# Routed attention and a SoLU layer on one core: the first pair's values loaded later, eight score tiles kept in a weight's place, and another order of the first 50 microseconds

## The chip, the core and the metric

The kernel runs on one core of a Trainium2 chip. A core has a matrix engine (TensorE, called PE), a vector engine (VectorE, DVE), an engine for activation functions (ScalarE, ACT), a general engine (GpSimd, POOL) and an engine that here only starts DMAs (SyncE, SP). Each takes its instructions in the order in which they were issued to it; between engines they wait on semaphores. Data lies in SBUF (128 partitions) and, for the results of PE, in PSUM (banks of 512 f32 for each partition). The metric is the device time of one execution, in microseconds (us); smaller is better.

## The reference

Four batches, eight heads, 768 tokens, head dimension 64. Each query and each key is assigned to the nearest of 16 centroids of its head; a query attends only to keys of its own cluster. The result goes through a layer with a softmax-weighted activation and a layer norm.

```python
q_assign = argmax(einsum('bhsd,hcd->bhsc', q_n, c_n))     # k_assign likewise; c_n: centroids at unit length
mask = q_assign[:, :, :, None] == k_assign[:, :, None, :]
attn = softmax(where(mask, q @ k.T / sqrt(64), -1e9))
x = (attn @ v)                                            # as 3072 tokens x 512
h = x @ w_in                                              # 512 x 1024
solu = h * softmax(h)
out = ((solu - mean) / sqrt(var + 1e-6) * g_ln) @ w_out   # 1024 x 512
```

## The kernel before

The kernel works on pairs of heads, `b.p` (batch, pair): 0.0 is the first pair. All its work is cut into small named pieces, and the class `Weave` holds, for each engine, a hand-written queue of the kinds of pieces (`ORDER`). A piece of a kind is taken in the order in which it was added. `AWAY` moves single pieces from their default engine to another. So the order of every engine's instructions is fixed text; the costs given to `add` only serve to merge the queues into one program.

The pieces of batch 0, in the order of one pair's life, with their lines:

- `ld`, `lv` (SP): the DMAs of queries and keys (`load_tokens` L367 for pair 0.0, `load_apart` L373 for the other three) and of values (`load_v` L526). `lo`, `li`, `lg` (SP) load w_out, w_in and g_ln. In the kernel before, the DMA of the first pair's values stands fixed in the code at L811, behind the loads of pair 0.0.
- `tp` (PE, L383): three f32 transposes of a half of q or k into one of the three banks of the PSUM region `hreg`, which the pieces use in turn. `xa` (DVE or ACT, L390) copies that bank out to `xt`; the third `tp` behind waits for it. `tp0.1.1.0` is pair 0.1, side 1 (keys; 0 is queries), half 0.
- `ca` (POOL, ACT or DVE, L424): casts `xt` to bf16 in `qk`.
- `cl` (PE, L439), `tb`, `mx`, `oh`, `ot` (all DVE, L457 to L495): scores against the centroids, transposed back, maximum, one-hot, transposed. Pair 0.0 has these twice, one for each half of its tokens. `pl` (POOL or DVE, L499) places the one-hot rows below the cast rows of `qk`; `bl` (L522) blanks 16 rows. `cp`, `cb`, `cq`, `cf` make two forms of the centroids; `zo` clears a tile once.
- `S` (PE, L595): one bank of scores, 128 keys x 384 queries (pair 0.0) or 512 columns (the others), into one of three PSUM banks; it needs the `E` three banks before. `S4.0` is bank 0 of unit 4. Banks 0 to 23 are pair 0.0 (units 0 to 3), S4.0 is bank 24.
- `E` (ACT, L604): the exponential of that bank into a bf16 tile `e`. There are 9 such tiles, so the tenth `E` waits for the `V` that read the first.
- `V` (PE, L616): six matmuls of one 128-query block with the values in `v1`, which `cv` (POOL or DVE, L532) cast and `z` (POOL) completed. `N` (DVE, L629) divides by the sum; the next group's `V` waits for it, since there is one PSUM tile `ops`.
- `su`, `me` (PE), `sk`, `ce` (DVE): sums and centring of w_out. `wi` (POOL, L552): casts one 128-row slice of w_in, 128x1024, to `w_in_sb`. `h`, `y` (PE, L709, L763) are the two matmuls of the second layer, `hm`, `u`, `bn` (DVE) and `ex` (ACT) its activation. `fl` and `wm` (PE, L818) are matmuls on zeros that nobody reads.

From about 46 us on, scores, values and the second layer are interleaved up to the end.

Of the kernel before, what the change touches and what calls it, by code (L numbers as in the profile page):

```python
# [22 lines left out]
class Weave:  # L23
# [6 lines left out]
        ld4 lv si ld4 lv lg ld4 lv2 ld4 lo2 ld4 lo ld3 lo ld3 li4 tx ld3 lv3 tx ld4 tu ld9 lv ld tu  # L30
        tx ld3 tu ld3 ou ld2 ou ld tu ld12 tu ld4 lv ld2 ou tx ld3 tu ou ld2 tx lv ld tu ld4 tx ld
        tu ou2 ld lv ld4 tu ld4 tu ld ou ld7 pl ou ld lv2 ld3 tu lv tx ou tu lv pl ld4 ou2 tx lv tu
        tx ou tu pl2 tu2 tx tu tx ou2 tx ou tu tx2 ou tu2 ou2 tu2 ou6
    """
    ORDER["POOL"] = """
        po z ca2 pl2 cv z bl pl2 ca z ca pl2 ca z2 ca3 cv ca cv ca pl3 sg ca cv2 pl3 ca2 gs pl ca cv
        ca wi ca pl2 wi3 bl ca pl2 cv at cv pl ca pl al bl at cv ca pl ca pl cv ca3 al at ca al ca
        at ca pl2 bl cv pl2 ca4 at ca2 al ca pl2 bl pl2 cv2 ca3 al at pl2 bl pl2 ca pl al ca3 at cv
        at pl ca pl2 ca2 pl al cv2 bl cv2 pl2 ca pl al pl at al at pl2 ca3 at al bl cv pl2 bl cv2
# [130 lines left out]
def kernel(  # L170
# [15 lines left out]
    P = 128  # L186
# [1074 lines left out]
```

## Time and profile before

| | |
|---|---|
| median of three runs | 225.12 us (225.0 to 227.68) |
| the profiled execution | 225.3 us |
| its span, first to last instruction | 223.3 us (2.0 us lie around it) |
| PE, DVE, ACT, POOL busy | 216.1, 196.8, 192.0, 127.7 us |
| granted PE clock | 0.999 |

How to read it: the times are of one execution. A row gives the start, the time, the engine, the line of the code, the operation, the tile written and the tiles read, the number of instructions, and in brackets how long the engine had been idle before and what ended that. Neighbours with the same form are merged into one row. A busy PE is not PE at its peak: a matmul's row holds the way through the array too, so a single matmul of 384 columns shows 0.33 us where a chain of them advances by 0.16 to 0.17 us.

### The profile page before, as it was taken

How to read it: one execution, taken by the hardware profiler on the slowest of the kernel's cores; microseconds unless marked ns; L12 is line 12 of the kernel's file. 1: busy time of each engine (PE TensorE's matmuls, PEld its weight loads, DVE VectorE, ACT ScalarE, POOL GpSimd, SP SyncE). 2: the span in 40 equal slices, each digit the busy share in tenths (PEclk: the TensorE clock that was granted, in tenths of full speed). 3: DMA queues.
4: the chain of work that ended last, by engine and by line, in shares of the span. 5: the costliest groups of instructions: out<-in, count | busy, mean ns of one | idle time of the engine just before them, and what ended most of it. 6: DMA issues, size and time to landing. Idle time of an engine off the chain costs nothing.

```text
span 223.3 us, 6607 instructions
## 1 busy us (share of the span) xinstructions
PE 216.1 (97%) x2420; PEld 147.7 (66%) x2420; DVE 196.8 (88%) x359; ACT 192.0 (86%) x372; POOL 127.7 (57%) x247
## 2 busy tenths in 40 slices
PE   6899999999999999999999999999999999999994
PEld 2576656677667678776577667777677777755452
DVE  3899898899999989999998999887999889888982
ACT  3689999999998999998889899999999998983362
POOL 3489843864794999547678534943895403022331
PEclk9999999999999999999999999999999999999999
DMA  7997999999897989898999999299930534486723
GB/s 152 330 310 156 259 186 270 274 265 192 143 214 137 220 142 162 170 191 182 188 243 150 152 187 216 72 219 191 235 63 15 92 61 129 93 145 159 181 85 120
DMA packets 125679, 38.80 MB, mean 174 GB/s; under 512 B 115016, under 2 KB 121168, under 8 KB 125648
## 3 DMA queue, kind: packets, MB, share of 16 engines
q1 hardware_dynamic: 123904, 37.87, 79.6%
q10 hardware_dynamic: 1744, 0.52, 1.0%
q8 instruction: 19, 0.31, 0.6%
q14 instruction: 12, 0.10, 0.1%
HBM read 23.11 MB, written 6.29 MB: 132 GB/s over the span
## 4 chain that ended last, share of the span: by engine, by line
PE 88%; ACT 5%; issue 2%; DMA 2%; DVE 1%; SPq 1%; POOL 0%; ACTq 0%; DVEq 0%; POOLq 0%
PE sps L602 28%; PE hreg L711 19%; PE yps L775 17%; PE ops L625 15%; PE csc L451 4%; ACT e L608 4%; DMA raw<-in_q_dram 2%; PE hreg L387 1%; PE hreg L575 1%; PE hreg L775 1%; PE csc L446 1%; SPq L370 0%; ACT xt L394 0%; PE hreg L585 0%; PE utp L699 0%
## 5 line engine op out<-in xcount | busy, mean ns | idle before, releaser
L608 ACT ACTIVATE e<-sps 128x512 bf16<-128x512 f32 (+1 forms) x294 | 151.0, 598 | 12.1 <-PE sps L602 10.2
L602 PE MATMUL sps<-qk 80*128 80x256 bf16 (+5 forms) x636 | 93.8, 264 | 1.7 <-POOL qk L515 0.7
L602 PEld LDWEIGHTS <-qk 80*128 80x128 bf16 (+1 forms) x636 | 60.2, 121 | 27.9 <-issue 9.0
L625 PEld LDWEIGHTS <-e 128*128 128x128 bf16 x1152 | 50.4, 97 | 12.3 <-issue 1.9
L625 PE MATMUL ops<-v,e 128*128 128x65 bf16 x1152 | 55.0, 193 | 0.0
L711 PE MATMUL hreg<-w_in_sb,xT 128*128 128x512 bf16 x192 | 52.9, 379 | 0.0
L775 PE MATMUL yps<-w_out_c,uT 128*128 128x512 bf16 x184 | 48.5, 379 | 0.0
L730 DVE TENSOR_TENSOR u<-e_sb,hreg 128x1024 bf16<-128x1024 bf16 (+1 forms) x25 | 29.1, 1168 | 5.2 <-ACT e_sb L723 5.1
L515 POOL COPY qk<-oht 32x384 f32<-32x384 f32 (+1 forms) x50 | 24.9, 498 | 15.3 <-DVE oht L495 13.0
L741 DVE BATCH_NORM_STATS2 bs<-u 128x6 f32<-128x512 bf16 x48 | 31.5, 677 | 0.1
L717 DVE TENSOR_REDUCE nmax<-hreg 128x1 f32<-128x1024 f32 x24 | 29.0, 1210 | 2.6 <-PE hreg L711 2.2
L723 ACT ACTIVATE e_sb<-hreg,nmax 128x1024 bf16<-128x1024 f32 x24 | 26.9, 1120 | 4.5 <-DVE nmax L717 4.4
L434 POOL CAST qk<-xt 64x768 bf16<-64x768 f32 (+1 forms) x31 | 25.9, 837 | 5.1 <-DVE xt L394 3.6
L775 PEld LDWEIGHTS <-uT 128*128 128x128 bf16 x200 | 18.3, 97 | 11.8 <-issue 0.3
L757 POOL TENSOR_SCALAR esq<-es,mv 128x1 f32<-128x1 f32 x24 | 8.6, 358 | 29.2 <-DVE mv L745 21.0
L436 POOL TENSOR_SCALAR qk<-xt 64x768 bf16<-64x768 f32 (+1 forms) x28 | 23.0, 822 | 1.7
L711 PEld LDWEIGHTS <-xT 128*128 128x128 bf16 x192 | 16.7, 97 | 9.4 <-issue 0.6
L408 DVE STREAM_TRANSPOSE xt<-raw 128x768 f32<-128x768 f32 x24 | 22.6, 953 | 0.3 <-DMA w_g<-in_moe_w_out_dram 0.2
L751 POOL TENSOR_SCALAR es<-esum 128x1 f32<-128x1 f32 x24 | 5.3, 223 | 25.9 <-ACT e_sb L723 25.4
L650 DVE TENSOR_TENSOR x<-ops,den 128x256 bf16<-128x256 f32 (+1 forms) x39 | 18.9, 486 | 1.3
L533 POOL CAST v<-vf 128x384 bf16<-128x384 f32 x27 | 13.6, 518 | 2.2 <-DMA vf<-in_v_dram 1.5
L760 POOL TENSOR_TENSOR alpha<-esq,halves 128x1 f32<-128x1 f32 x24 | 13.5, 563 | 2.0
(80 smaller groups left out, 164.5 us busy)
## 6 DMA issues: line engine op xcount, KB each, us to landing
vf<-in_v_dram SPq DMA_DIRECT2D x16, 384.0 KB, 4.9
out_dram<-y SPq DMA_DIRECT2D x23, 256.0 KB, 2.6
raw<-in_q_dram SPq DMA_DIRECT2D x50, 96.0 KB, 3.6
raw<-in_k_dram SPq DMA_DIRECT2D x50, 96.0 KB, 3.1
w_g<-in_moe_w_out_dram SPq DMA_DIRECT2D x4, 512.0 KB, 5.2
w_st<-in_moe_w_in_dram SPq DMA_DIRECT2D x4, 512.0 KB, 6.1
raw<-in_q_dram SPq DMA_DIRECT2D x3, 384.0 KB, 6.2
raw<-in_k_dram SPq DMA_DIRECT2D x3, 384.0 KB, 6.9
```

Of the source, the lines that this page charges most:

```text
L434: VEC[e].tensor_copy(dst, src)
L436: VEC[e].tensor_scalar(dst, src, scalar1=inv_C, scalar2=1.0, op0=Alu.mult, op1=Alu.mult)
L515: ins = VEC[e].tensor_copy(dst.bitcast(F32), src.bitcast(F32).unsqueeze(1) .to_broadcast([NB, 2, n // 2]))
L602: nc.tensor.matmul(sps_[n, k][:, c0:c0 + w], side(b, h // 2, 1, h % 2, keys)[r], side(b, h // 2, 0, h % 2, slice(s0 * P, s0 * P + w))[r])
L608: nc.scalar.activation(es[n, k][:, :w], sps_[n, k][:, :w], Act.Exp, scale=exp_scale, bias=-exp_scale)
L625: nc.tensor.matmul(opss[g][:, s, :VW], es[n, k][:, c0:c0 + P], v1[slot(b, h // 2)][:, h % 2, kt, :VW], start=(kt == 0), stop=(kt == n_t - 1))
L711: uses(nc.tensor.matmul(hreg[:, at(f, f2)[1], :], xTs[f][:, dc, :], w_in_sb[:, dc, f2 * FF2:(f2 + 1) * FF2], start=(dc == 0), stop=(dc == ...
L717: uses(nc.vector.tensor_reduce(ff[f, "nmax"][:], pair_of(f), axis=AXY, op=Alu.max, negate=True), *both(f))
L723: uses(nc.scalar.activation(ff[f, "e"][:], pair_of(f), Act.Exp, bias=ff[f, "nmax"][:], accum_out=ff[f, "esum"][:]), *both(f))
L730: uses(nc.vector.tensor_tensor(ff[f, "u"][:, at_], ff[f, "e"][:, at_], pair_of(f)[:, at_], op=Alu.mult), *banks)
L741: nc.vector.bn_stats(ff[f, "bs"][:, f2, :], ff[f, "u"][:, f2, :])
L775: ins = nc.tensor.matmul(dst, ff[f, "uT"][:, at(f, f2)[0] * (n_fc // 2) + c, :], w_out_c[:, fc, cols], start=(fc == chunks[0]), stop=(fc = ...
```

## The change

1. The DMA of the first pair's values is no longer fixed behind the loads of pair 0.0; it is a piece of SP's queue (`lv0.0`), and stands behind the loads of pairs 0.1 and 0.2.
2. The exponentials of banks 0 to 7 no longer go to the 9 tiles `e`, but to the eight 128x512 halves of `w_in_sb`, which stands empty until `wi` fills it. So the first `E` that waits for a `V` is the eighteenth. Each `wi` now waits for the `V` of the units whose banks lie there.
3. The queues of all five engines have another order up to about S19.0, and some pieces another engine. Behind that point all queues are what they were.

What the queues hold up to bank 24, spelled out (PE from the first scores, DVE from the first token copies, ACT from its first copies, POOL):

```
PE before   ... cl0.0.1 fl x4 S0.0 S0.1 S0.2 tp0.1.0.0 tp0.1.0.1 S1.0 S1.1 tp0.1.1.0 S1.2 cq S0.3 tp0.1.1.1 S0.4 S0.5
            tp0.2.0.0 tp0.2.0.1 S1.3 S1.4 V0.0-2 S1.5 cl0.1 S2.0 tp0.2.1.0 tp0.2.1.1 V1.0-2 S2.1 gt S2.2 tp0.3.0.0 S2.3
            tp0.3.0.1 S2.4 S2.5 cl0.2 S3.0 S3.1 V2.0 V2.1 S3.2 V2.2 S3.3 S3.4 tp0.3.1.0 S3.5 S4.0 tp0.3.1.1 S4.1
PE after    ... cl0.0.1 fl x3 tp0.1.0.0 tp0.1.0.1 S0.0 S0.1 S0.2 cq tp0.1.1.0 tp0.1.1.1 S1.0 S1.1 S1.2 tp0.2.0.0
            tp0.2.0.1 S0.3 S0.4 cl0.1 S0.5 S1.3 S1.4 tp0.2.1.0 tp0.2.1.1 S1.5 S2.0 gt S2.1 V0.0 S2.2 V0.1 V0.2 V1.0 S2.3
            V1.1 S2.4 S2.5 V1.2 cl0.2 S3.0 tp0.3.0.0 S3.1 V2.0 V2.1 S3.2 S3.3 V2.2 tp0.3.0.1 S3.4 S3.5 tp0.3.1.0 S4.0 S4.1
DVE before  cn cb xa0.0.0.1 ca0.0.1.0.0 tb0.0.0 mx oh ot pl pl tb0.0.1 mx oh ot xa0.1.0.0 xa0.1.0.1 xa0.1.1.0 bl0.0.1
            cf cv0.0.0 xa0.1.1.1 zo xa0.2.0.0 xa0.2.0.1 tb0.1 ca0.1.1.0 mx oh gk N0 ot0.1 tb0.2 pl0.1.0.0 mx0.2 ...
DVE after   cn xa0.0.0.0 xa0.0.1.0 cb tb0.0.0 mx oh ot pl tb0.0.1 mx oh ot xa0.1.0.0 xa0.1.0.1 cf xa0.1.1.0 xa0.1.1.1
            pl xa0.2.0.0 tb0.1 cv0.0.0 mx xa0.2.0.1 oh gk xa0.2.1.0 ot0.1 N0 tb0.2 xa0.3.0.0 mx0.2 pl0.1.1.0 ...
ACT before  wa xa0.0.0.0 xa0.0.1.0 ca ca xa0.0.1.1 ca ca, E of banks 0-11, xa0.2.1.0 xa0.2.1.1, E 12-17, xa0.3.0.0, E 18 ...
ACT after   wa xa0.0.0.1 xa0.0.1.1 ca ca ca ca ca, E of banks 0-14, xa0.2.1.1, E 15-17, ca0.2.0.0, E 18 ...
POOL before ca ca pl pl cv0.0.1 bl0.0.0 pl pl ca0.0.1.1.1 ca0.1.0.0 pl pl ca0.1.0.1 ...
POOL after  ca ca pl pl pl bl0.0.0 ca0.0.1.1.0 pl zo pl bl0.0.1 ca0.1.0.0 pl ca0.1.0.1 cv0.0.1 ...
```

Further on, DVE takes `xt1.0.0` (the first transpose of batch 1's queries) ahead of `pl0.2.0.0` and `tb0.3`, where it stood behind them; `wi1` goes from POOL to DVE; and SP issues the first half-megabyte load of w_out (`lo0`) ahead of the last quarter of the load `ld1.0.0`, and `lv0.3` behind it.

The diff, cut to its core:

```diff
     ORDER["SP"] = """
-        ld4 lv si ld4 lv lg ld4 lv2 ld4 lo2 ld4 lo ld3 lo ld3 li4 tx ld3 lv3 tx ld4 tu ld9 lv ld tu
...
+        ld4 si ld3 lg ld lv2 ld lv ld4 lo ld lv ld3 lo ld lo ld5 lo ld3 li4 tx ld4 lv3 tx ld3 tu ld9
...
     ORDER["PE"] = """
-        wm tp2 cp tp cl tp fl5 cl fl4 S3 tp2 S2 tp S cq S tp S2 tp2 S2 V3 S cl S tp2 V3 S gt S tp S
...
+        wm tp2 cp tp cl tp fl5 cl fl3 tp2 S3 cq tp2 S3 tp2 S2 cl S3 tp2 S2 gt S V S V3 S V S2 V cl S
...
     ORDER["ACT"] = """
-        wa xa2 ca2 xa ca2 E12 xa2 E6 xa E58 ex E12 ex E8 ex E8 ex E3 sc E5 ca E2 ex E25 ex E9 sc E6
...
+        wa xa2 ca5 E15 xa E3 ca E58 ex E12 ex E8 ex E8 ex E3 sc E5 ca E2 ex E25 ex E9 sc E6 ex E5 sc
...
+    EARLY = 2 * n_dc
+
...
     def expo(n, k):
         w = wide(n, k)
-        es[n, k] = ep.tile([P, 512], BF16, name="e")
+        i = BANKS.index((n, k))
+        es[n, k] = (w_in_sb[:, i // 2, i % 2 * FF2:(i % 2 + 1) * FF2] if i < EARLY else
+                    ep.tile([P, 512], BF16, name="e"))
...
-    load_v(0, 0)
...
-            add(f"lv{t}", "SP", 0.0, -1990, lambda e: None, [], last_ld[-1:], move=1.3)
+            add(f"lv{t}", "SP", 0.6, -40, lambda e: load_v(0, 0), [], ["si"], move=1.3, bulk=True)
...
-        if i >= ring_e:
+        if i >= EARLY + ring_e:
...
+    held = sorted({f"V{n}.{j}" for n, k in BANKS[:EARLY] for j in range(len(UNITS[n]["subs"]))})
     for dc in range(n_dc):
...
-        add(f"wi{dc}", "POOL", 1.04, 28 + dc, (lambda e, dc=dc: cast_w_in(dc, e)), [f"li{dc}"],
+        add(f"wi{dc}", "POOL", 1.04, 28 + dc, (lambda e, dc=dc: cast_w_in(dc, e)), [f"li{dc}"] + held,
             also={"DVE": 0.62})
```

More of the change, by code (lines that the diff above doesn't have):

```diff
@@ new lines @@
+        V S h S2 V3 S2 V h S2 h V2 S y3 S2 h3 S3 y V3 h V S2 V2 S cl S3 h2 S2 V3 S y2 S V h2 S V y2
+        S h S V h S2 h S y3 S2 y V3 h S3 cl V2 S V S y S2 y2 S3 V3 S y S2 V3 S2 cl S V S2 V2 S h S2
+        V2 S V S h S2 V2 cl V2 S3 y2 S V S2 V y S2 y V2 S3 h2 S V h S h S2 V h S V S V y2 S h V y2
+        S2 V S h3 S cl V S2 V2 S h V cl S3 h2 V y V S3 y2 V S h V3 S y S h S2 h2 S3 V2 y h S V S2 y
+        V3 y S3 h3 y S3 V3 S h S V S V cl S V S h S cl V2 S3 y V2 S y S2 y V2 S3 h y V S3 V h V2 S3
@@ L68 @@
+        u bn2 hm sc u N ag2 bn tx hm bn sc u bn ag hm bn tu ag u2 bn2 ag sc
     """
     ORDER["ACT"] = """
-        wa xa2 ca2 xa ca2 E12 xa2 E6 xa E58 ex E12 ex E8 ex E8 ex E3 sc E5 ca E2 ex E25 ex E9 sc E6
-        ex E5 sc E2 ex E9 ex E8 ex E9 sc E6 ex E18 ex E21 ex E5 sc E3 ex E9 ex E7 sc E2 ex E7 ex E8
-        ex E7 ex E6 sc E ex E2 sc E3 ex E2 sc ex sc ex sc ex sc tu3 sc2 oz
+        wa xa2 ca5 E15 xa E3 ca E58 ex E12 ex E8 ex E8 ex E3 sc E5 ca E2 ex E25 ex E9 sc E6 ex E5 sc
+        E2 ex E9 ex E8 ex E9 sc E6 ex E18 ex E21 ex E5 sc E3 ex E9 ex E7 sc E2 ex E7 ex E8 ex E7 ex
@@ L1194 @@
     for name, eng, busy in (("cn", "DVE", 4.66), ("wa", "ACT", 4.3), ("po", "POOL", 3.7),
-                            ("si", "SP", 3.95)):
-        add(name, eng, busy, -1000, lambda e: None, [], ["lv0.0"] if eng == "SP" else [])
+                            ("si", "SP", 3.45)):
+        add(name, eng, busy, -1000, lambda e: None, [], last_ld[3:4] if eng == "SP" else [])
     LO, LI = 12, 0
```

72 lines of the change are left out of this document (33 added, 39 removed).

## The prediction

> **What bounds the kernel now.** The page has PE busy for 216.1 of 223.3 us. So I first read the busy time of each engine in stretches, to see where time could be lost at all.
>
> ```profile
> 10.00:22.00 12.00, 11.71 (x130) 8.26 (x130) 11.24 (x27) 10.57 (x27) 10.74 (x22) 1.00 0.96 251
> 22.00:46.00 24.00, 23.59 (x324) 15.76 (x325) 21.61 (x43) 22.66 (x45) 15.74 (x24) 1.00 1.01 244
> 53.00:223.30 170.30, 166.77 (x1854) 115.27 (x1852) 152.39 (x260) 147.04 (x279) 94.51 (x179) 1.00 0.76 152
> ```
>
> The columns after the stretch are its length and the busy time of PE, weight loads, DVE, ACT and POOL; the last is what the DMAs moved in GB/s. From 53 us on PE is busy 166.77 of 170.30 us, and the queues there stay as they are. So the change is worth what it shifts the moment at which PE enters that part; a us won or lost before goes through to the end. Before it, three engines are nearly full at once: from 22 to 46 us PE 98%, ACT 94%, DVE 90%. A busy PE there includes matmuls that wait, so I read the chain that ended last, from its start.
>
> ```profile
> 6.64 0.56 DVE xt L394
> 7.46 0.30 DVE cst L460
> ...
> 9.15 0.36 POOL qk L515
> ...
> 9.56 0.35 POOL qk L515
> ...
> 9.96 0.65 PE sps L602 x3
> 10.61 0.66 PE hreg L387 x6
> ...
> 14.82 0.78 PE csc L446 x8
> ...
> 19.58 0.37 ACT xt L394
> 19.95 0.69 ACT e L608 x2
> ...
> 21.96 0.39 PE sps L602 x2
> ```
>
> Up to 9.96 us it is one thread: copy, cast, transpose back and one-hot on DVE, placement on POOL, S0.0. Then PE's own queue, in which six transposes take 0.66 us and a `cl` 0.78; then ACT; at 21.96 us S4.0 (bank 24). There the first pair is through, and both queues have the same work behind them: all V of units 0 to 2, and one `tp` left. I therefore carry the new order by hand as far as E24 and compare. Before, E18 starts at 19.95 and six exponentials of 0.40 us bring E24 to 22.35 us, as S4.0 (21.96, and 0.36 from a score's start to its exponential, 9.96 to 10.32 below) does.
>
> **The change, part by part.** The rows for the pieces:
>
> ```profile
> 3.46 0.49 SPq L528 DMA_DIRECT2D vf<-in_v_dram  x1
> ...
> 3.99 0.47 SPq L375 DMA_DIRECT2D raw<-in_q_dram  x1
> ...
> 5.28 0.52 PE L387 MATMUL hreg<-ident_f,raw 128*128 128x128 f32 x3 [0.64 <-DMA raw<-in_k_dram]
> ...
> 5.83 0.48 ACT L394 COPY xt<-hreg 128x384 f32<-128x384 f32 x1 [0.68 <-PE hreg L387]
> 5.94 0.29 DVE L876 TENSOR_TENSOR c_bd<-cps,own 128x128 f32<-128x128 f32 x1 [1.15 <-PE cps L865]
> ...
> 6.54 0.53 PE L451 MATMUL csc<-xt,c_bd 128*32 128x192 f32 x8
> ...
> 7.00 0.55 PE L387 MATMUL hreg<-ident_f,raw 128*128 128x128 f32 x3
> ...
> 8.15 1.06 ACT L432 ACTIVATE qk<-xt 64x384 bf16<-64x384 f32 x2
> ...
> 9.04 0.58 DVE L515 COPY qk<-oht 32x192 f32<-32x192 f32 x2
> ...
> 10.32 3.56 ACT L608 ACTIVATE e<-sps 128x384 bf16<-128x384 f32 x9 [1.11 <-PE sps L602]
> ...
> 11.15 1.45 DVE L394 COPY xt<-hreg 128x384 f32<-128x384 f32 x3
> ...
> 12.85 0.67 PEld L387 LDWEIGHTS hreg<-ident_f,raw 128*128 128x128 f32 x6 [0.21 <-DVE xt L394]
> ...
> 12.94 0.42 DVE L869 TENSOR_TENSOR w_out_c<-cps,own 128x256 f32<-128x256 f32 x1
> ...
> 14.60 1.26 ACT L608 ACTIVATE e<-sps 128x384 bf16<-128x384 f32 x3 [0.72 <-PE ops L625]
> ...
> 15.24 1.03 SPq L400 DMA_DIRECT2D raw<-in_q_dram  x2
> ...
> 16.98 2.60 ACT L608 ACTIVATE e<-sps 128x384 bf16<-128x384 f32 x6
> ```
>
> *Up to S0.0: a loss.* The first keys' transposes end at 5.80, set by a DMA that the change leaves alone. Their copy now runs on DVE, 0.56 instead of 0.48 us, to 6.39; `cb` (0.29), which stood in DVE's idle time, follows it, to 6.68. `cl0.0.0` begins 0.22 us after its last input (6.31 to 6.53), at 6.90 instead of 6.54. DVE no longer does a copy and a cast ahead of `tb0.0.0`, but it has to wait for that `cl` (0.53, and some 0.08): 7.50 instead of 7.38. One-hot and transposes as before, so placement begins at 9.27. POOL now has three of the four placements instead of two. At 0.41 from start to start and 0.35 for the last it ends at 10.44; S0.0 starts at **10.49 instead of 9.96**. ACT: `tp0.0.1.1` is 0.46 behind `cl0.0.0`, its copy ends at 8.4, and five casts of 0.53 follow instead of four with a gap: E0 starts at **11.1 instead of 10.32**.
>
> *PE's transposes ahead of S0.0: a gain.* `tp0.1.0.0` and `tp0.1.0.1`, 0.66 us together by the chain, go where PE waited for the placement. Their data comes earlier:
>
> ```profile
> vf<-in_v_dram SPq DMA_DIRECT2D x1, 384.0 KB, 4.9
> raw<-in_q_dram SPq DMA_DIRECT2D x1, 384.0 KB, 5.4
> ```
>
> These two were issued at 3.46 and 3.99, so they landed at 8.36 and 9.39; with the values gone, pair 0.1 takes the first place, 8.4 us. The values become the fifth such transfer: 8.36 + 4 x 1.03 = 12.5 us. Their `V0.0` stands behind S2.1, about 16.3 us, and DVE takes their cast at about 15.2; nothing waits, and if that cover of 2.7 us were gone, the `V` would be late one for one, with only seventeen tiles of `E` to cover it.
>
> *PE's waits on DVE ahead of S1.0 and S0.3: a loss.* Each `tp` waits for the copy three before it. DVE has one placement (0.30) less ahead of `tb0.0.1`, so `xa0.1.0.0` starts at 11.0, `xa0.1.0.1` 0.48 later, `cf` takes 0.42, `xa0.1.1.0` runs from 12.4 to 12.9, `xa0.1.1.1` to 13.4. `tp0.1.1.1` needs the first of these, ended 11.55, and 0.25 for the hop (12.60 to 12.85): 11.8. Behind it in the queue S1.0 starts at 12.13, E3 at 12.5; E0 plus three is 12.3: 0.2 lost. `tp0.2.0.1` needs `xa0.1.1.0`: 13.15; S0.3 at 13.5, E6 at 13.87 instead of 13.7: 0.17. Then S0.4, `cl0.1` 0.78, S0.5 at 14.6: E8 at 14.97 instead of 14.67: 0.3.
>
> *The ring of E: a gain.* Before, E9 waited 0.72 us for the first `V` (row at 14.60), and two copies stood on ACT between E11 and E12. Both waits go; E9 follows E8 at 15.37 and E12 starts at 16.57 instead of 16.98. What is late next is ACT itself: behind E14 a copy (0.48), behind E17 the cast `ca0.2.0.0`, for which ACT has no row. Its bounds are the half-size cast, 0.53, and twice that, 1.06; an exponential grows by 0.11 from 384 to 512 columns (0.40 to 0.51: 3.56 us for 9, and 5.55 for 11 further below), so 384 more cost 0.33, and I take 0.85. E18 is then at 16.57 + 2.40 + 0.48 + 0.85 = 20.3 (19.95 before), **E24 at 22.7 (22.35 before): +0.35 us**, 0.05 to 0.55 by the bounds of the cast.
>
> *Does S4.0 come in time?* It needs `pl0.1.1.0`, now on DVE behind `mx0.2`:
>
> ```profile
> 15.69 0.58 DVE L460 STREAM_TRANSPOSE cst<-csc 128x384 f32<-128x384 f32 x1 [0.15 <-PE csc L446]
> ```
>
> ```profile
> 20.68 0.55 DVE L473 TENSOR_REDUCE mx<-cst 128x24 f32<-128x384 f32 x1
> ```
>
> From `tb0.1` to the end of `mx0.2` DVE took 5.54 us with one placement in it; now that placement is the last of the stretch, a cast of values replaces one of keys, and three copies of 0.48 come in: 7.0. From `cl0.1`'s end, 14.7, that is 21.7; S4.0 is due at 22.3. It holds, by 0.6 us.
>
> *The waits of `wi`.* They name `V` of units 0 and 1, done by 19 us; the casts run after 39: free. Two of them now stand on POOL behind three placements, and one on DVE:
>
> ```profile
> 42.53 3.14 POOL L553 CAST w_in_sb<-w_st 128x1024 bf16<-128x1024 f32 x3
> ...
> 44.59 5.55 ACT L608 ACTIVATE e<-sps 128x512 bf16<-128x512 f32 x11 [0.16 <-PE sps L602]
> ...
> 45.96 0.60 PE L711 MATMUL hreg<-w_in_sb,xT 128*128 128x512 bf16 x2
> ```
>
> The last ended at 45.67, 0.3 us ahead of the first `h`. One cast less on POOL (1.05), one placement more (about 0.5): it ends some 0.5 us earlier, so I cost it at nothing; with a late `ot1.0` it costs up to 0.5.
>
> ```profile
> L434 POOL CAST qk<-xt 64x768 bf16<-64x768 f32 (+1 forms) x31 | 25.9, 837 | 5.1 <-DVE xt L394 3.6
> ```
>
> ```profile
> 33.83 0.74 DVE L434 CAST qk<-xt 64x768 bf16<-64x768 f32 x1
> 34.11 1.15 POOL L434 CAST qk<-xt 64x768 bf16<-64x768 f32 x1
> ```
>
> The same POOL cast took 0.84 us in the mean of the page and 1.15 beside a DVE cast. The Trainium skill, "SBUF — State Buffer", section "SBUF: two separate sides", says why that can be: DVE, in its modes that use both ports, and GpSimd share one port pair, and "the loser fully blocks". It speaks against `wi1` on DVE beside `wi0` and `wi2` on POOL: by it POOL would be held for up to that cast's length, estimated at 1.0 us (0.74 us for 768 columns, 1024 now), and the first `h` would come up to 0.5 us late; by what the rows show, 0.31, nothing.
>
> **Sum.** +0.35 us at E24, the same work behind it: +0.3. The profiled execution would be 225.6; against the median, 0.2 below that execution, **225.4 us**.
>
> **Rivals.** *Faster: the new waits on DVE aren't there.* If each copy is done before PE asks, ACT alone sets E24: 11.1 + 9.6 + 0.48 + 0.85 = 22.0, and 21.8 if E0 follows S0.0 at 10.85: 0.35 to 0.6 won, with the small cast 0.9. That speaks for it that the chain from 9.96 to 15.6 is PE's own queue, which loses 0.66 us of transposes; against it that DVE is busy 11.24 of 12 us there. 224.5, down to 224.2. Chance 0.26.
>
> *Slower: DVE is the bound at S4.0.* In `tb0.1` to `pl0.1.1.0` DVE also waits: `N0` for V1.2, which PE now does behind S2.5, `tb0.2` for `cl0.2` behind that. It decides from a slip of 0.6 us. Two waits of a `cl` (0.78) and an E pitch (0.40), with hops of 0.25 each, are 1.7: +0.35 + 1.1 = +1.5, 226.6. Chance 0.19.
>
> *Slower: `xt1.0.0` blocks DVE.* It now stands ahead of `pl0.2.0.0`, due at about 26.0; its last load, the second of the pair in the row at 15.24, was issued at 15.75 and took 6.6:
>
> ```profile
> raw<-in_q_dram SPq DMA_DIRECT2D x2, 96.0 KB, 6.6
> ```
>
> It landed at 22.3; 512 KB of w_out ahead of it, at 250 GB/s, make it 24.4. Only past 27 us would it cost. 226.4 if it lands at 28.3; chance 0.05.
>
> *The change doesn't do what it says:* were `w_in_sb` ordered as one tile, the `V` would only wait for E7, which ends before they start, so the time is that of the forecast. `wi` late by the port, +0.5, 225.9: 0.03.
>
> **How the numbers follow.** My forecast, 224.9 to 226.0 around 225.4, has 0.43; the rivals have 0.26, 0.19, 0.05 and 0.03; 0.04 is left for a stall in the new order that I didn't find. The range reaches over the two larger rivals with their own spread, 224.0 to 226.9; outside lie that stall, the far ends of both, and a landing later than 28.3, together some 0.15. 2%, 4.5 us, is about what a measurement of this kernel can tell from no change, and no case but that stall comes near: slower 0.04; faster 0.01, for PE's loss before 53 us cannot shrink by that much; within 0.95.
>
> **What would show it.** S0.0 at 10.5 and E0 at 11.1 us; no ACT wait on `ops` at E9; PE's transposes waiting on DVE `xt` ahead of S1.0 and S0.3; E12 near 16.6, E24 near 22.7; the stretch from 53 us as long as before, 0.3 us later. I am wrong if E24 is off by more than 0.6 us, or if the shift there isn't the shift at the end.

## The result

The kernel after has a median of **226.57 us** (225.63 to 228.68, 22 runs), the kernel before on the same chip 225.22 us (224.99 to 228.5, 22 runs); the ratio is **1.0044 [1.0024, 1.0063]**. The ratio is taken over the runs and not from the two medians (they alone would give 1.006), and it leaves out before's longest run, 228.5 us, as a slow one. By it the change costs about 1.0 us, within 2%. The profiled execution took 226.7 us with a span of 224.6 us; before's took 225.3 with 223.3.

The same stretches as before, in the kernel after (columns as in the first fence of the prediction):

```profile
10.00:22.00 12.00, 11.91 (x130) 8.10 (x129) 11.56 (x25) 11.60 (x29) 10.69 (x23) 1.00 0.98 285
22.00:46.00 24.00, 23.01 (x298) 14.54 (x296) 21.38 (x41) 21.64 (x44) 14.46 (x24) 1.00 0.96 224
53.00:224.60 171.60, 167.85 (x1864) 116.11 (x1863) 153.71 (x261) 148.06 (x281) 94.25 (x180) 1.00 0.78 153
```

Up to 22 us PE and ACT are fuller than before (11.91 against 11.71 us, 11.60 against 10.57). From 22 to 46 us both lose: PE 23.01 instead of 23.59, ACT 21.64 instead of 22.66. So something is won early and lost in the middle. The timeline of the kernel after, by start and time of each group, says when:

```profile
10.22 0.65 PE L603 MATMUL sps<-qk 80*128 80x384 bf16 x3
10.82 3.35 ACT L611 ACTIVATE w_in_sb<-sps 128x384 bf16<-128x384 f32 x8
11.29 0.31 PEld L386 LDWEIGHTS hreg<-ident_f,raw 128*128 128x128 f32 x3 [0.22 <-DVE xt L393]
11.68 0.73 PE L603 MATMUL sps<-qk 96*128 96x384 bf16 x3
12.16 0.70 PEld L386 LDWEIGHTS hreg<-ident_f,raw 128*128 128x128 f32 x6 [0.22 <-DVE w_out_c L871]
12.94 0.49 PE L603 MATMUL sps<-qk 80*128 80x384 bf16 x2
```

```profile
14.52 2.79 ACT L611 ACTIVATE e<-sps 128x384 bf16<-128x384 f32 x7 [0.34 <-PE sps L603]
...
18.86 0.84 ACT L431 ACTIVATE qk<-xt 64x768 bf16<-64x768 f32 x1
19.61 5.41 ACT L611 ACTIVATE e<-sps 128x384 bf16<-128x384 f32 x12
25.66 0.60 ACT L611 ACTIVATE e<-sps 128x512 bf16<-128x512 f32 x1 [0.64 <-PE sps L603]
```

```profile
21.50 0.63 PE L603 MATMUL sps<-qk 80*128 80x256 bf16 x4
...
23.92 1.33 PE L445 MATMUL csc<-xt,w_out_c 128*32 128x384 f32 x8
```

S0.0 starts at 10.22, 0.26 later than before, and S4.0 at 21.50, 0.46 *earlier*. E18 (19.61) and six exponentials of 0.40 us put E24 at 22.0; in the kernel before it starts at 22.45 (the prediction's 22.35 was carried by hand). Behind that, ACT waits 0.64 us at 25.66 for PE, whose `cl0.3` took 1.33 us from 23.92; in the kernel before:

```profile
24.44 0.85 PE L446 MATMUL csc<-xt,w_out_c 128*32 128x384 f32 x8
```

And then (timeline of the kernel after, 24 to 48 us):

```profile
24.41 0.14 PEld L445 LDWEIGHTS csc<-xt,w_out_c 128*32 128x32 f32 x2 [0.33 <-DVE xt L393]
```

```profile
37.41 0.14 PEld L574 LDWEIGHTS hreg<-w_g,w_out_c 128*32 128x32 f32 x4 [0.49 <-DMA w_g<-in_moe_w_out_dram]
...
42.29 1.04 POOL L552 CAST w_in_sb<-w_st 128x1024 bf16<-128x1024 f32 x1
42.54 1.34 DVE L552 CAST w_in_sb<-w_st 128x1024 bf16<-128x1024 f32 x1
...
45.79 0.54 PE L628 MATMUL ops<-v,e 128*128 128x65 bf16 x12 [0.40 <-DVE x L653]
...
47.21 0.60 PE L714 MATMUL hreg<-w_in_sb,xT 128*128 128x512 bf16 x2
```

Three waits follow one another: `cl0.3` for copies on DVE, `su1` for the last part of w_out (`lo3`), and a `V` for `N`, which on DVE stands behind `wi1`. The first `h` is at 47.21 instead of 45.96, **1.25 us late**, and the span ends 1.3 us late. The chain that ended last runs through the cast:

```profile
41.85 0.75 DVE w_out_c L587
42.60 1.27 DVE w_in_sb L552
43.88 1.31 DVE w_out_c L587 x2
...
45.32 0.43 DVE x L653
```

So 0.46 us is won up to S4.0, and 1.71 us is lost between S4.0 and the first `h` (25.71 us from one to the other, 24.00 before).

### The profile page after: what moved, and what is told of

Same layout as the page of the kernel before. It is cut to its first block, busy times and chain, and to the rows that moved or that the text cites. A ratio compares the mean times of both kernels' runs of the same rounds, so it can differ in the third digit from the quotient of the medians.

```text
span 224.6 us, 6600 instructions
## 1 busy us (share of the span) xinstructions
PE 218.0 (97%) x2419; PEld 148.3 (66%) x2419; DVE 198.8 (88%) x358; ACT 191.9 (85%) x371; POOL 126.7 (56%) x249
## 4 chain that ended last, share of the span: by engine, by line
PE 89%; DVE 4%; issue 2%; ACT 1%; DMA 1%; POOL 0%; SPq 0%; DVEq 0%; ACTq 0%; POOLq 0%
PE sps L603 28%; PE hreg L714 18%; PE yps L778 17%; PE ops L628 15%; PE csc L450 4%; PE hreg L386 2%; DMA raw<-in_k_dram 1%; PE csc L445 1%; PE hreg L574 1%; ACT e L611 1%; DVE w_out_c L587 1%; PE hreg L778 1%; DVE w_in_sb L552 1%; DVE xt L407 1%; DVE oht L494 0%
## 5 line engine op out<-in xcount | busy, mean ns | idle before, releaser
L611 ACT ACTIVATE e<-sps 128x512 bf16<-128x512 f32 (+1 forms) x286 | 147.9, 601 | 12.0 <-PE sps L603 11.0
L628 PEld LDWEIGHTS <-e 128*128 128x128 bf16 x1128 | 49.7, 97 | 12.6 <-issue 2.7
L628 PE MATMUL ops<-v,e 128*128 128x65 bf16 x1128 | 54.4, 193 | 0.4 <-DVE x L653 0.4
L514 POOL COPY qk<-oht 32x384 f32<-32x384 f32 (+1 forms) x50 | 24.4, 487 | 20.6 <-DVE oht L494 18.4
L433 POOL CAST qk<-xt 64x768 bf16<-64x768 f32 (+1 forms) x30 | 24.3, 810 | 4.7 <-DVE xt L393 1.7
```

Of the source, the lines that this page charges most:

```text
L433: VEC[e].tensor_copy(dst, src)
L514: ins = VEC[e].tensor_copy(dst.bitcast(F32), src.bitcast(F32).unsqueeze(1) .to_broadcast([NB, 2, n // 2]))
L611: nc.scalar.activation(es[n, k][:, :w], sps_[n, k][:, :w], Act.Exp, scale=exp_scale, bias=-exp_scale)
L628: nc.tensor.matmul(opss[g][:, s, :VW], es[n, k][:, c0:c0 + P], v1[slot(b, h // 2)][:, h % 2, kt, :VW], start=(kt == 0), stop=(kt == n_t - 1))
```

## The experiments

All kernels were timed against the kernel before on the same chip. The table has, from the profile of each: how long the last load of pair 0.0 (keys, issued on SP at 2.9 to 3.1 us) took to land, the start of S0.0, the time of `oh0.1` (the one-hot of pair 0.1) on DVE, the start of S4.0, the time from there to the first `h`, and from that to the end of the span.

| kernel | median (lowest) us | ratio to before [95%] | load | S0.0 | oh0.1 | S4.0 | to `h` | to the end |
|---|---|---|---|---|---|---|---|---|
| before | 225.22 (224.99) | | 3.3 | 9.96 | 0.60 | 21.96 | 24.00 | 177.3 |
| after | 226.57 (225.63) | 1.0044 [1.0024, 1.0063] | 4.2 | 10.22 | 0.79 | 21.50 | 25.71 | 177.4 |
| lo3_early | 226.22 (225.44) | 1.0043 [1.0014, 1.0072] | 3.8 | 11.33 | 1.17 | 23.21 | 25.22 | 178.0 |
| wi1_pool | 226.15 (225.16) | 1.0031 [1.0007, 1.0055] | 3.8 | 10.25 | 0.79 | 21.52 | 24.53 | 177.3 |
| both | 226.27 (225.08) | 1.0037 [1.0012, 1.0063] | 4.2 | 10.18 | 0.79 | 21.45 | 24.54 | 178.4 |
| early_only | 226.09 (225.87) | 1.0035 [1.0009, 1.0062] | 3.8 | 11.35 | 1.17 | 23.32 | 25.45 | 177.4 |
| late_only | 226.12 (225.46) | 1.0033 [1.0006, 1.0059] | 3.3 | 9.73 | 0.61 | 21.73 | 24.68 | 178.1 |
| tp_back | 227.01 (225.90) | 1.0068 [1.0041, 1.0095] | 4.0 | 9.92 | 1.16 | 22.03 | 25.21 | 177.5 |
| after_fill | 226.43 (225.50) | 1.0026 [0.9997, 1.0055] | 4.5 | 10.09 | 1.17 | 22.00 | 25.22 | 177.5 |
| before_fill | 226.20 (225.10) | 1.0015 [0.9970, 1.0060] | 3.5 | 9.92 | 0.60 | 21.91 | 24.01 | 177.4 |
| xa_first | 226.25 (224.69) | 1.0010 [0.9972, 1.0048] | 4.6 | 10.47 | 1.17 | 22.35 | 24.63 | 177.9 |
| xa_first_lo3 | 226.26 (225.17) | 1.0023 [0.9992, 1.0054] | 4.0 | 10.35 | 0.79 | 21.62 | 24.51 | 178.5 |
| ring_only | 225.58 (224.87) | 0.9992 [0.9954, 1.0030] | 3.5 | 9.88 | 0.60 | 21.88 | 24.16 | 177.3 |
| dve_light | 226.49 (225.03) | 1.0032 [0.9997, 1.0067] | 4.9 | 10.69 | 1.17 | 22.91 | 23.93 | 177.3 |

The times of one kernel lie up to 4.0 us apart, and the median of before differs between the chips (225.22 to 225.51). So kernels are compared by the ratio, within its interval, and the mechanism is read from the profiles, one execution of each kernel.

**lo3_early, wi1_pool, both.** The two late waits, undone one at a time and together.

```diff
 SP     ... lo2
+lo3
 ld1.1.0.0 ld1.1.0.1 ld1.1.0.2 ld1.1.0 ld1.1.1.0
-lo3
 ld1.1.1.1 ...
```

> The changed kernel with one DMA moved: the last load of w_out (lo3) is issued right behind lo2, ahead of the five loads ld1.1.0.* and ld1.1.1.0, behind which it stood. Late-loads theory: the changed kernel's lead of 0.46 us at S4.0 is lost where the second su waits for lo3 (its eight matmuls took 1.69 instead of 1.07 us), and sk and the DVE chain behind it are late with it. Then su1 takes 1.07 us again, sk starts about 0.6 us earlier, and the time falls by about 0.6 us, to within 0.2% of the kernel before. Cast theory: the loss is wi1 on DVE (1.34 us beside POOL's cast) ahead of N7, for which V16 waits; wi1 needs its load anyway, so this run gains 0.2 us at most. Early-order theory (the loss is made ahead of S4.0): no change, and S4.0 where it was, 21.5 us.

```diff
-POOL   ... wi0 wi2 wi3        DVE ... ce0 wi1 ce1 ce2
+POOL   ... wi0 wi1 wi2 wi3    DVE ... ce0 ce1 ce2
```

> The changed kernel with the cast wi1 back on POOL, between wi0 and wi2. Cast theory: N7 ends about 1.3 us earlier, V16 no longer waits for DVE (0.40 us in the changed kernel), and the time falls by 0.4 to 0.6 us. Late-loads theory: su1 still waits 0.6 us for lo3, POOL's four casts now end later than 46.25 us, where three ended, since they wait for their loads too; the first h takes over the wait, and the time falls by 0.2 us at most, or not at all.

> Both edits: lo3 behind lo2, and wi1 on POOL. If the late load and the cast on DVE are in series on one chain (su1, sk, ot1.0, two transposes, wi1, N7, V16), the gains add up, about 1.0 to 1.2 us off the changed kernel, and the time is 0.1 to 0.3 us below the kernel before, since S4.0 comes 0.46 us earlier there. If one hides the other, the sum is no more than the larger of the two alone.

With `lo3` early, `su1` takes 1.07 us and S4.0 to `h` is 25.22 us, 0.49 less than in after; that is the wait. With `wi1` on POOL it is 24.53 us. In that profile `su1` doesn't wait either:

```profile
24.43 0.14 PEld L445 LDWEIGHTS csc<-xt,w_out_c 128*32 128x32 f32 x2 [0.33 <-DVE xt L393]
```

```profile
36.80 1.06 PE L574 MATMUL hreg<-w_g,w_out_c 128*32 128x512 f32 x8
...
41.71 3.99 POOL L552 CAST w_in_sb<-w_st 128x1024 bf16<-128x1024 f32 x4
...
46.05 0.60 PE L714 MATMUL hreg<-w_in_sb,xT 128*128 128x512 bf16 x2
```

So `lo3` lands in time in some executions and not in others: of the six profiles in which it stands where after has it, `su1` took 1.69 us in after, 1.22 in late_only and 1.06 in the other four. Among those in which it lands in time, the cast on DVE costs 25.22 - 24.53 = **0.69 us** (lo3_early against wi1_pool), of which 0.1 may come from the late `oh0.1` of lo3_early: xa_first, which has it, takes 0.12 us more from S4.0 to `h` than xa_first_lo3. Four casts on POOL (3.99 us) are quicker for PE than three there and one on DVE. The times don't confirm the gain: the ratios 1.0043, 1.0031 and 1.0037 can't be told from after's 1.0044, and `both` is not below before, as was expected. In `both` the first `h` is as early as in wi1_pool, and 1.1 us goes behind it, where the chain of both has

```profile
54.89 4.03 DMA raw<-in_k_dram
...
58.94 0.98 DVE xt L407
```

The load was issued 8.90 us behind the first `h` (54.89 - 45.99), in wi1_pool 8.04 us. SP's rows show what came before it, in wi1_pool and in both:

```profile
49.13 3.58 SPq L399 DMA_DIRECT2D raw<-in_k_dram  x3
```

```profile
48.98 4.52 SPq L399 DMA_DIRECT2D raw<-in_k_dram  x3
```

Issuing three loads held SP 0.9 us longer, and DVE's transpose, and with it `u` and PE, waited. Of the ten profiles with the new late order of SP, five end 177.9 to 178.5 us behind the first `h`, and in each of these the chain that ended last runs through this load and the 0.98 us transpose; in the other five it runs through neither, and they end after 177.3 to 177.5 us, the four with the old order after 177.3 to 177.4. The time of these three issues alone doesn't sort them: it is 3.28 us in late_only, which is late, and 4.18 in after, which isn't.

**early_only.** The early order alone, the old one behind it.

```diff
 PE to tp0.3.1.1, DVE to N1, ACT to E3.0, POOL to ca0.2.1.1, SP to lv0.3: the order of after
-behind these: the order of after
+behind these: the order before (with wi1 on POOL)
```

> The changed kernel's queues up to S4.1 and its neighbours (DVE up to N1, POOL up to ca0.2.1.1, SP up to lv0.3, ACT up to E3.0), and behind them the order and the engines of the kernel before: lo1 to lo3 among the loads as they were, wi1 on POOL, xt1.0.0 behind pl0.2.1.1 and tb0.3. If the early order is a gain and the loss lies behind S4.0, S4.0 is at 21.5 us, the second su doesn't wait, the first h starts 0.3 to 0.5 us earlier than in the kernel before, and the time is 0.3 to 0.5 us below it. If the early order itself costs something that shows only later (the values loaded late, the loads shifted), it is 0.3 us above or more.

Slower than before by 0.35%, though nothing of the late part is in it. From S4.0 to `h` it takes 1.45 us more than before: `cl0.3` takes 1.43 us, and two `V` wait 0.18 and 0.36 us for `N` on DVE. Its profile caught an execution like that of lo3_early, in which PE ran at half its rate to 10 us (timeline of lo3_early; the kernel after has 0.71 for the five, and 0.61 for the `csc`):

```profile
8.24 1.27 PE L822 MATMUL idle_p<-w_out_c 128*128 128x256 bf16 x5
9.44 0.87 PE L450 MATMUL csc<-xt,c_bd 128*32 128x192 f32 x8
```

That gave the theory that the early order, with more f32 transposes ahead of S0.0, suffers from PE's slow first microseconds. The next four kernels were made for it.

**late_only, tp_back, after_fill, before_fill.**

```diff
 early part: the order before; banks 0 to 7 in w_in_sb
-behind it: the order before
+behind it: the order after
```

> The mirror of early_only: the kernel before up to the second pair's norms (S4.0 and tp0.3.1.1 on TensorE, N1 on VectorE, E3.0 on ScalarE, lv0.3 on SyncE, values of the first pair loaded first), with the eight banks in w_in_sb, and behind that the order of the kernel after: lo3 behind ten key and query loads, wi1 on VectorE, S9.0 ahead of su0. Theory 1 (the early order costs the time, because it runs on a slow TensorE): no change against before, 225.0 to 225.5, S4.0 at 21.9 as before, and runs no more spread than those of before. Theory 2 (what stands behind S4.0 costs it: lo3's wait in su1 of 0.49 and wi1's 0.5 to 1.0 us on VectorE): +0.6 to +1.3 us, 225.9 to 226.5, h0 at 46.6 or later. If both hold in part, +0.3.

```diff
-PE     fl x3 tp0.1.0.0 tp0.1.0.1 S0.0 S0.1 S0.2 cq
+PE     fl x3 S0.0 S0.1 S0.2 tp0.1.0.0 tp0.1.0.1 cq
```

> The kernel after with the two turns tp0.1.0.0 and tp0.1.0.1 back behind S0.2, where before has them; all else as after. Theory 1 (slow TensorE ahead of the first scores): these six f32 turns, 0.82 us at full rate and 1.6 at half rate, leave the path to S0.0, so S0.0 comes 0.4 to 0.8 us earlier where it waits for TensorE, at 9.9 as in before, and the time is 225.7 to 226.2 against 226.57 for after, with fewer runs above 226.5. Theory 2 (what stands behind S4.0): the median stays at 226.2 to 226.6. A third case: the turns fall behind S0.2 onto a path that ScalarE waits on, S4.0 is no earlier than 21.9 and nothing is won.

```diff
-        wm tp2 cp tp cl tp fl5 cl fl3 ...
+        wm tp fl2 tp cp tp cl fl tp fl5 cl fl3 ...
```

> The kernel after with three more of the idle 256-column matmuls on TensorE, two in its wait for the second load (behind tp0.0.0.0) and one ahead of tp0.0.1.1, so that it never stands still between 1.2 and 9 us. Theory 1 (the moment at which TensorE comes to full rate, which the waits of 0.3 and 0.2 us delay, makes the spread): full rate from 5 to 8 us in every execution, none with a 0.87 csc at 9.4; the median 0.3 to 0.7 us below after's, 225.8 to 226.3, and the upper runs gone. If the moment does not hang on these waits: the same median and spread as after, 226.2 to 226.6, or up to 0.3 more by the added 0.25 us each.

> The kernel before with the same three idle matmuls at the same places. Theory 1: before is less open to a slow TensorE (S0.0 waits for GpSimd's qk until 9.96, with 0.73 us in hand), so its median moves by under 0.2 us, and its upper quarter (226 to 227) thins out. If the upper runs of before have another cause, a load's landing for one, they stay: median 225.0 to 225.5 with a quarter of runs above 226.

late_only costs +0.68 us from S4.0 to `h` and +0.75 behind it in its profile, and 0.33% in the ratio. So each half of the order by itself is slower than before by about as much as the two together (1.0035, 1.0033 and 1.0044). The intervals, some 0.0025 to either side, don't tell whether what the halves cost adds up.

The theory of the slow PE did not hold as the cause of the later S4.0. With idle matmuls in its waits PE was at full rate from 5.1 us at the latest in both profiles (three transposes in 0.49 us instead of 0.87 in after; timeline of after_fill):

```profile
5.11 0.49 PE L386 MATMUL hreg<-ident_f,raw 128*128 128x128 f32 x3
```

It got there by 5.3 us in before, both and tp_back, too, which have no such matmuls. The medians are 226.43 us for after_fill, where the theory asked for 225.8 to 226.3, and 226.20 for before_fill, whose upper runs (up to 228.12) stayed. A gain of after_fill is not excluded: its ratio is 1.0026 [0.9997, 1.0055], and none of its 12 runs is above 227.19, while four of after's 22 are. tp_back, which frees the path to S0.0 and starts it at 9.92, has the highest median and ratio of all, and S4.0 0.5 us later than in after. Two profiles of 14 show PE slow to 10 us, and there S0.0 is 1.1 us later than in after. That something else is at work, after_fill and tp_back show: S0.0 is *earlier* in both than in after, and S4.0 is later. The rows of POOL and DVE in the kernel after, and then in after_fill:

```profile
15.52 1.93 POOL L435 TENSOR_SCALAR qk<-xt 64x768 bf16<-64x768 f32 x2
```

```profile
15.97 0.79 DVE L478 TENSOR_TENSOR w_out_c<-cst,mx 128x384 bf16<-128x384 f32 x1
```

```profile
15.15 1.80 POOL L435 TENSOR_SCALAR qk<-xt 64x768 bf16<-64x768 f32 x2
```

```profile
16.19 1.17 DVE L478 TENSOR_TENSOR w_out_c<-cst,mx 128x384 bf16<-128x384 f32 x1
```

The one-hot `oh0.1` runs beside two scalings on POOL. Where it starts 0.45 us behind the first of them, it ends 0.41 us after that one (16.35 to 16.76) and takes 0.79 us; where it starts 1.04 us behind it, at the begin of the second, it ends 0.41 us after the second (16.95 to 17.36) and takes 1.17. In the four profiles with before's early order it takes 0.60 or 0.61 (in before it ends 0.41 us after a cast of POOL, 17.40 to 17.81). The table shows what follows: with 0.79, S4.0 is 11.27 or 11.28 us behind S0.0 in all four profiles; with 1.17 (1.16 in tp_back) it is 11.9 to 12.2 us in all six; before's order has 12.0 in all four. So the gain of the new order, 0.7 us from S0.0 to S4.0, was there only where `oh0.1` fell well against POOL.

Which of the two comes is visible one piece earlier, where DVE and POOL each cast a half of the first pair's values (the kernel after, and then after_fill):

```profile
14.81 0.32 DVE L532 CAST v<-vf 128x384 bf16<-128x384 f32 x1
14.82 0.67 POOL L532 CAST v<-vf 128x384 bf16<-128x384 f32 x1
```

```profile
14.63 0.50 POOL L532 CAST v<-vf 128x384 bf16<-128x384 f32 x1
14.84 0.51 DVE L532 CAST v<-vf 128x384 bf16<-128x384 f32 x1
```

In after the two start together and POOL's is the longer one. In after_fill POOL, whose placements for S0.0 ended 0.19 us earlier, starts 0.21 us ahead of DVE, and DVE's is the longer one. DVE itself is no earlier, since its pieces there wait for PE's `cl0.1` (13.39 in after_fill, 13.36 in after). So an earlier S0.0 can make S4.0 later: it brings POOL forward, and not DVE. All four profiles with 0.79 show the first picture and five of the six with 1.17 the second; in tp_back POOL's cast was over, at 15.02, before DVE's began at 15.07. No run moved this piece by itself.

With the late one-hot S4.0 has to wait (after_fill):

```profile
20.87 0.82 POOL L433 CAST qk<-xt 64x768 bf16<-64x768 f32 x1
20.88 1.02 DVE L506 COPY qk<-w_out_c 16x384 f32<-16x384 f32 x1
22.00 0.60 PE L603 MATMUL sps<-qk 80*128 80x256 bf16 x4 [0.31 <-POOL qk L433]
```

The bracket names POOL's cast, but that had ended at 21.69; what ended just before S4.0 is the placement `pl0.1.1.0` on DVE, at 21.90. In all six profiles with 1.17 this placement took 1.02 us and S4.0 started 0.10 or 0.11 us behind its end; in the four with 0.79 it took 0.73 or 0.74, and S4.0 did not wait for it.

The Trainium skill, "SBUF — State Buffer", section "SBUF: two separate sides", calls the port pair of DVE and GpSimd "an exclusive lock, not a bandwidth split" for the whole instruction of the one that starts first, where DVE's instruction uses both ports or reads two inputs in SBUF. These rows agree, and so does `wi1`: beside POOL's cast from 42.29 to 43.33 it ended at 43.88, 0.55 us after it. One row in tp_back does not: a scaling of POOL that starts at 15.05, 0.02 us ahead of DVE's cast, took 1.03 us instead of 0.83, and DVE's cast 0.32.

The second thing in the early part is the load:

```profile
raw<-in_k_dram SPq DMA_DIRECT2D x1, 96.0 KB, 3.3
```

```profile
raw<-in_k_dram SPq DMA_DIRECT2D x1, 96.0 KB, 4.2
```

```profile
raw<-in_k_dram SPq DMA_DIRECT2D x1, 96.0 KB, 4.9
```

This is the last load of pair 0.0, issued at about 3.1 us, in before, after and dve_light. Behind it SP issues values in before, and queries and keys in after. It took 3.3 to 3.5 us to land in the four profiles with the values behind it, 3.8 to 4.9 in the ten without. PE's last transposes ahead of `cl0.0.1` wait for it, up to 0.73 us; where it landed latest, at 7.8 and 8.0 us (xa_first, dve_light), S0.0 came at 10.47 and 10.69. That the queries behind it are the cause was not tried by itself.

**xa_first, xa_first_lo3, dve_light.** Where the lead of S4.0 goes: `cl0.3` waits for two copies which DVE does behind a cast of values.

```diff
-DVE    ... oh0.2 cv0.2.0 xa0.3.1.0 xa0.3.1.1 ot0.2 N1      (on wi1_pool)
+DVE    ... oh0.2 xa0.3.1.0 xa0.3.1.1 cv0.2.0 ot0.2 N1
```

> wi1_pool (the kernel after with wi1 on GpSimd) and in VectorE's order the cast cv0.2.0 behind the copies xa0.3.1.0 and xa0.3.1.1 instead of ahead of them. Theory A (the lead of 0.46 us at S4.0 is given back at cl0.3, where TensorE waits for these copies: csc 1.33 us from 23.94 in wi1_pool, 0.85 from 24.44 in before): the csc takes 0.85 again, S6.0 starts near 24.7 instead of 25.2, ScalarE waits no 0.64 us at 25.7, h0 at 45.5 to 45.7 instead of 46.05, and the fastest runs are 0.3 to 0.5 us under those of wi1_pool, at 224.8. Theory B (ScalarE or a load sets the pace behind S4.0): csc 0.85, but h0 at 46.0 and 225.2 for the fastest, as wi1_pool. In both the upper runs stay, since nothing is done about VectorE being full from 10 to 22 us.

> The same with lo3 issued right behind lo2. Theory A: as xa_first where lo3 lands in time, and without the runs in which su1 waits for it (0.49 us in the profile of after): median 0.1 to 0.4 below xa_first's, su1 1.07 without a wait. Theory B: as both, 226.2 to 226.3. If lo3 ahead of the key and query loads makes those land late (in both, batch 1's xt waited for a key load at 55 us): median no lower than xa_first's, and a wait on raw in the chain behind 50 us.

The wait at `cl0.3` went, 0.85 us as before. The next row is the next wait (xa_first_lo3, PE):

```profile
24.03 0.85 PE L445 MATMUL csc<-xt,w_out_c 128*32 128x384 f32 x8
...
26.06 0.73 PE L628 MATMUL ops<-v,e 128*128 128x65 bf16 x18 [0.41 <-DVE x L653]
```

The `V` waits for `N1`, which stands behind the same work on DVE; S4.0 to `h` stays at 24.51. In xa_first the same `V` waits 0.52 us. Its two fastest runs, 224.69 and 224.83 us, lie where theory A put them, but those of xa_first_lo3, from 225.17, where theory B did, so the times decide nothing. The rows point at DVE's amount of work and not at this order. From 10 to 28 us DVE is busy 17.44 of 18 us in after and 16.30 in before (the third busy time in each row, before and then after):

```profile
10.00:28.00 18.00, 17.61 (x213) 12.56 (x213) 16.30 (x38) 16.30 (x38) 15.91 (x31) 1.00 0.98 251
```

```profile
10.00:28.00 18.00, 17.60 (x203) 11.90 (x202) 17.44 (x36) 16.88 (x39) 15.54 (x31) 1.00 0.96 258
```

```diff
-DVE    ... oh0.2 cv0.2.0 xa0.3.1.0 xa0.3.1.1 ot0.2    POOL ... cv0.1.1 cv0.2.1 ca0.2.1.0 ca0.2.1.1 gs pl0.2.1.0   (on both)
+DVE    ... oh0.2 xa0.3.1.0 xa0.3.1.1 ot0.2            POOL ... cv0.1.1 cv0.2.0 ca0.2.1.0 ca0.2.1.1 gs cv0.2.1 pl0.2.1.0
```

> The kernel after with three of its moves undone: wi1 on GpSimd, lo3 right behind lo2, and the cast cv0.2.0 (0.98 us on VectorE, ahead of the copies that cl0.3 waits for) on GpSimd, where cv0.2.1 stood; cv0.2.1 goes behind gs, into GpSimd's wait of 0.79 us at 24.6. Theory A (VectorE is the bound from S4.0 to 28 us: in xa_first_lo3 the wait at cl0.3 went, and TensorE waited 0.41 us for N1 on VectorE at 26.06 instead, h0 at 46.13): with 0.98 us less on VectorE both waits go, csc 0.85 near 23.9, no wait of the ops on x at 26, the lead of 0.46 us at S4.0 holds, h0 at 45.5 to 45.7, the fastest runs 0.3 to 0.5 below those of both and before (224.5 to 224.7). Theory B (the pace behind S4.0 is set by ScalarE or by loads): both waits may go, but h0 stays at 46.0 and the fastest runs at 225.1. In both, where VectorE's one-hot at 16 us takes 1.17 instead of 0.79 beside GpSimd, S4.0 comes at 22.0, so upper runs and a median near 225.8 to 226.2 remain.

```profile
25.32 0.85 PE L445 MATMUL csc<-xt,w_out_c 128*32 128x384 f32 x8
...
26.77 0.74 PE L628 MATMUL ops<-v,e 128*128 128x65 bf16 x18
```

With 0.98 us taken from DVE neither wait is left, and S4.0 to `h` is 23.93 us, 0.6 less than in both, 0.7 less than in xa_first, which has the late `oh0.1` too, and as short as before's. So theory A holds for this stretch, in this one profile. The first `h`, at 46.84, and the fastest run, 225.03 us, are not where it put them: in this execution the load took 4.9 us and `oh0.1` 1.17, S4.0 came at 22.91, and the runs spread as in the other kernels with this early order.

**ring_only.** The banks in `w_in_sb` alone.

```diff
 before, and
-        es[n, k] = ep.tile([P, 512], BF16, name="e")
+        es[n, k] = (w_in_sb[...] if i < EARLY else ep.tile([P, 512], BF16, name="e"))
```

> The kernel before with nothing changed but the first eight banks of E in w_in_sb (and so the ring of E tiles free for longer). E9 then no longer waits 0.72 us for the first V, if that wait was for the ring; ScalarE's next wait is the two copies xa0.2.1.0 and xa0.2.1.1 (16.24) or the scores. Expected: E9 to E11 up to 0.7 us earlier, but S4.0 waits for GpSimd and E18 behind a copy, so S4.0 at 21.5 to 21.96 and the time 0 to 0.4 us below before: 224.9 to 225.3. If the loss of after came from the banks themselves (waits of wi on the V of units 0 and 1, or a tile ordered as one), this kernel would be slower than before by 0.5 us or more, with GpSimd's wi casts later than 42.5.

```profile
13.26 2.01 ACT L612 ACTIVATE e<-sps 128x384 bf16<-128x384 f32 x4
16.16 0.86 ACT L394 COPY xt<-hreg 128x384 f32<-128x384 f32 x2 [0.89 <-PE hreg L387]
```

E9's wait of 0.72 us for the first `V` is gone, and 0.89 us of waiting for PE's transposes stand behind E11 in its place (0.38 before); S4.0 is at 21.88 as before. 0.9992 [0.9954, 1.0030]: the ring alone shows neither a gain nor a cost. No kernel beat before beyond its interval.

## Why the prediction was right or wrong

225.4 us was forecast and 226.57 measured. It lies in the range, and on the side of the rivals that were slower, but the path to it was another one.

- *Up to S0.0: a loss.* Right in kind, sized too high in this profile: 10.22 instead of 10.49, E0 10.82 instead of 11.1. `cl0.0.0` was at 6.70, not 6.90, and the one-hot took 0.36 us instead of 0.42, so POOL's placements began at 9.03 and not at 9.27. What the step left out is that the *last* load of the pair also changes its neighbour; in xa_first and dve_light, where it landed latest, S0.0 is at 10.47 and 10.69.
- *Transposes ahead of S0.0: a gain.* PE's wait of 0.73 us ahead of S0.0 is gone, as meant, but what that gains is not shown. tp_back undoes the move, and is 0.5 us later at S4.0, but with the late `oh0.1`; after_fill, which has the move and the late `oh0.1`, is at 22.00, and tp_back at 22.03.
- *PE's waits on DVE.* The first is there: `tp0.1.1.1` waits 0.22 us for `xa0.1.0.0`, as forecast. The second wait of 0.22 us is for `cf`, at `tp0.2.0.0` and not at `tp0.2.0.1`, and costs PE nothing: the weights wait, but the transpose starts at 12.25, 0.16 us behind S1.2 (12.09), as in a chain.
- *The ring of E.* No wait on `ops` at E9, and 0.84 us for the cast on ACT against 0.85. But E24 was at 22.0, not 22.7: off by 0.7, beyond the 0.6 at which I said I was wrong, and a lead instead of a loss. The term that failed is DVE's start: its copies began 0.28 us earlier than forecast (10.72, not 11.0), PE went on 0.05 us behind the end of the first (11.23 to 11.29) where the sum had 0.25, and the second wait cost nothing. So S1.0 was at 11.68 instead of 12.13 and E12 at 16.05 instead of 16.57. The other 0.2 us are from E12 to E24, which took 5.93 us instead of 6.13.
- *S4.0 holds.* Right in this profile: PE did not wait there. In the six profiles with the late `oh0.1` it did, 0.11 to 0.39 us, and for `pl0.1.1.0` on DVE, the piece that this step looked at. The step took DVE's pieces at their lengths in before; in these six the one-hot took 0.4 us and the placement 0.3 us more than in after.
- *`wi` at nothing, with the port up to 0.5 and a chance of 0.03.* Wrong: up to 0.69 us. I looked at POOL, which would end earlier, and at POOL being held. The one that was held is DVE, and DVE carries `ce` and `N` behind it.
- *"The same work behind it".* **The step that failed.** The shift at E24 (-0.47 in the profiles) is not the shift at the end (+1.3). The same pieces stood in the queues, but DVE carried 1.1 us more up to 28 us and `wi1` later, and SP issued `lo3` 2 us later (32.18 against 30.12). Before, it landed 5.5 us after its issue, at 35.6, and `su1` started at 36.71: 1.1 us in hand, which I had not looked up. In the profile of after: +0.53 for DVE behind S4.0, +0.69 for `wi1`, +0.49 for `lo3`; with -0.46 up to S4.0, 1.25 us at the first `h`. These are differences between single profiles of four kernels.
- *The rivals.* "Faster" is what the profile shows up to S4.0. "DVE is the bound", priced at 226.6, has the right engine, and by chance the right time. In the profile of after not `pl0.1.1.0` at S4.0 decides, but the copies for `cl0.3` and `N` behind `wi1`. In the six profiles with the late `oh0.1`, `pl0.1.1.0` does hold S4.0, as the rival said, but for 0.4 us at most, where the rival asked for 1.1.

What stays open is how often each case occurs in the runs of after. Its lowest eight lie at 225.63 to 226.08, and its one profiled execution, 226.7 us, is not one of them. No kernel that undid a late wait was faster than after beyond the intervals, so that these waits make the median is argued from profiles and not shown by times.

## What to carry to other kernels

Where three engines are nearly full, price a move by what it adds to *each* of them up to the next point at which all queues join, and don't stop at the point where the new order ends: a lead there is worth nothing if the engine that took the work is full behind it. A piece on VectorE costs what stands behind it in its queue, not its own time, and beside GpSimd it can wait for nearly the whole instruction of that engine (`oh0.1` in after_fill, 0.76 of 0.83 us). And a gain that hangs on two engines missing each other by half a microsecond should be looked at in several profiles.

## What the runs showed of the hardware

- PE comes to full rate at a moment that varies from one execution to the next: five idle matmuls of 256 columns took 0.71 us in after at 7.79, and 1.27 in lo3_early at 8.24. The granted clock from 7.5 to 9.5 us reads 1.00 in both. The Trainium skill, "TensorE: Matmul & The Clock Gate", Part 1, says that the release is run-variable with a window of some 3.4 us; here it came between about 4 and 10 us. With idle matmuls in the waits it was there at 4.1 and 5.1 us in two profiles, but without them at 5.2 to 5.3 us in before, both and tp_back, so what they do is not shown.
- A DVE instruction beside POOL's took 0.60, 0.79 or 1.17 us by its place against POOL's, the same instruction on the same data; in before, after and after_fill it ended 0.41 us behind one of POOL's. Two casts that started within 0.01 us took 0.32 us on DVE and 0.67 on POOL; with POOL 0.21 us ahead they took 0.51 and 0.50.
- The same 96 KB load took 3.3 to 3.5 us to land where values followed it in SP's queue and 3.8 to 4.9 us where queries and keys did; the two orders differ in more than that, so this is not shown as the cause.
- Issuing a load can hold SP for microseconds: in after a single one of batch 1's query loads stood from 27.85 for 3.71 us, with `lo3` two places behind it.
